# One chunk of 512 query columns instead of two of 256 at the end of a two-layer attention and mixer kernel

## The chip, the cores and the metric

The kernel runs on one core of a Trainium2 chip. The metric is the time of one execution in microseconds of device time; lower is better. The core has five engines that this text speaks of: TensorE (PE in the profile, its weight loads PEld), VectorE (DVE), ScalarE (ACT), GpSimd (POOL) and SyncE (SP), which issues most transfers.

## What is computed

Two equal layers over an input of 2048 rows by 448 columns. Each layer is a 16-head attention block (head size 28) and a mixer with an MLP, both with layer norms and residuals. Cut to what matters:

```
def _A_ref(x, wqkv, wo):
    q, k, v = heads(x @ wqkv)
    scores = jnp.einsum("bhqd,bhkd->bhqk", q, k) * (Dh ** -0.5)
    p = _softmax(scores, axis=-1)
    o = jnp.einsum("bhqk,bhkd->bhqd", p, v)
    return merged(o) @ wo
def _B_ref(x, w1, w2, w3, w4):
    h = _gelu(_layernorm(x) @ w1)
    hs = shifted_by_rows(h) @ w2      # column groups shifted by -1, +1, -2, +2 rows
    x1 = x + hs
    return x1 + _gelu(_layernorm(x1) @ w3) @ w4
for layer in range(2):
    x = x + _A_ref(_layernorm(x), A_wqkv, A_wo)
    x = x + _B_ref(_layernorm(x), B_w1, B_w2, B_w3, B_w4)
```

The weights are the same in both layers; w3 is 448 by 1792, w4 1792 by 448.

## The kernel before

**Tiles and chunks.** The 2048 rows are 16 tiles of 128. The queries of a layer are cut into chunks of tiles by `CHUNKS` (line 542): three chunks of four tiles (512 columns), then two of two tiles (256 columns): tiles 12 and 13, and 14 and 15. The 16 heads are four head groups g of four heads j. `ORDER` (line 543) lists pieces of attention work, each a chunk with a range of key tiles; a piece times a head group is a segment, and there are 68 of them (32 in layer one, 36 in layer two). A chunk whose keys are cut into several pieces spills its partial sums to DRAM (`uscr`) between them; the last chunks are done in one piece.

**Blocks.** A segment is a row of blocks. A block is one bank of PSUM, 128 keys by 512 values: one key tile by 512 queries, or two key tiles by 256 queries (line 668). A layer has 1024 blocks whatever the chunks. `t_scores` (line 1629) lets TensorE write the scores of two or three blocks at a time into banks 0 to 2 and 3 to 5, `t_exp` (line 1740) lets ScalarE take one exponential over those banks (line 1754), and `t_pv` (line 1768) multiplies by the values into bank 7, whose content VectorE copies out at the end of the segment (line 1838, or 1840 where a partial sum is read back).

**Blocks on VectorE.** Some blocks are not given to ScalarE: VectorE computes their exponential by a polynomial in eight instructions (`d_first`, line 1582, and `d_chain`, line 1595). `ahead_of` (line 1640) chooses such a block some key tiles ahead of the stream, if a quota per pair of segments allows it (`R_RATE`, line 552, `D_RATE`, line 564), if VectorE's planned load is under a threshold (`XPAR` keys 'dt'), and if a buffer is free: two of `yd`, three of `fb`, four of `PD`, and some more in unused slots of `vaug`. These extra ones in layer two are open until the segment `XSHUT` = 4 * (number of pieces) - 7 = 61 starts (line 558; `t_extra`, line 1543); after that the same space, with slots of `kT`, can hold the hidden values of an MLP group (`h2W`, line 2152).

**Behind a chunk.** `t_norm` (line 1824) divides by the softmax sums: for most chunks through DRAM (SyncE sends sums, a reciprocal by VectorE, four transfers back), for the last chunk of layer two by small matmuls (`PENORM`, line 597). `t_outproj` (line 1904) applies wo. `t_mixA` (line 1968) norms, transposes and applies w1 with a gelu. `t_mixB` (line 2124) does an MLP group of `BGROUPS` (line 545): the token mix of each tile with w2 (`t_mixB1`, which needs its two neighbours' w1 results, so that groups lag a tile behind chunks), norm, transpose, w3 with a gelu; `t_w4` (line 2224) applies w4, and `t_store` (line 2248) sends the result out. Layer two's groups are tiles 0 to 2, 3 to 6, 7 to 10, 11 and 12, and 13 to 15, one for each chunk.

**Three forms of gelu.** ScalarE's exponential and its gelu need different tables. In the middle, the first gelu is made from a tanh, which shares the table of the exponential, with steps on VectorE and GpSimd (line 2030), and the MLP's gelu is saved up: VectorE copies w3's result out of PSUM (line 2196) and one long gelu runs over the whole group between two table loads (line 2220). For the last chunk of layer two (`direct`) and for whatever comes behind the last exponential (the event "tail"), ScalarE takes the gelu straight from PSUM (lines 2000 and 2192), the transposes are done by TensorE (line 1078) instead of by DMA, and the hidden values of a direct group lie in `PT`, the tile of the exponentials.

**Order.** Nothing is ordered by hand. Every step is a generator with a priority (`RANK`, line 562, smaller goes first; segments have priority 0 and 1), and a planner in the kernel (`Sched`, line 185) simulates the engines with rough costs and writes out each engine's instruction list: the instruction that can start first, then by priority. Each engine then runs its list in that order. `XPAR` (line 575) says among others for some steps whether GpSimd (0), VectorE (1) or the earlier one (2) does them. Where TensorE would be idle for long, the planner puts in filler matmuls (line 2267) to keep its clock up.

Of the kernel before, what the change touches and what calls it, by code (L numbers as in the profile page):

```python
# [538 lines left out]
        return max(self.cur.values())  # L539


CHUNKS = {0: [(0, 4), (4, 4), (8, 4), (12, 2), (14, 2)], 1: [(0, 4), (4, 4), (8, 4), (12, 2), (14, 2)]}
ORDER = {0: [(0, 0, 4), (1, 0, 4), (0, 4, 8), (0, 8, 16), (1, 4, 16), (2, 0, 16), (3, 0, 16), (4, 0, 16)], 1: [(0, 0, 7), (1, 0, 7), (0, 7, 11), (1, 7, 11), (0, 11, 16), (1, 11, 16), (2, 0, 16), (3, 0, 16), (4, 0, 16)]}
KC = {0: [(0, 4), (4, 4), (8, 4), (12, 4)], 1: [(0, 3), (3, 4), (7, 4), (11, 2), (13, 3)]}
BGROUPS = {0: [[[0, 1, 2]], [[3, 4, 5, 6]], [[7, 8, 9, 10]], [[11, 12]], [[13, 14, 15]]], 1: [[[0, 1, 2]], [[3, 4, 5, 6]], [[7, 8, 9, 10]], [[11, 12]], [[13, 14, 15]]]}
TR_T = 2.6
TRL_T = 5.4
PVB = 2
DPRIO = 2.5
DST = [0.2, 0.2, 0.336, 0.2, 0.336, 0.336, 0.2]  # L550
# [1820 lines left out]
```

## Time and profile before

| | us |
|---|---|
| median of two runs | 1025.47 (1025.05 to 1025.9) |
| the profiled execution | 1025.66 |
| its span, first to last instruction | 1023.9 |
| ScalarE busy | 973.6 (95%) |
| of it exponentials, 791 instructions | 877.8 |
| TensorE busy, fillers included | 973.4 (95%) |
| VectorE busy | 843.5 (82%) |
| GpSimd busy | 220.1 (21%) |
| mean granted TensorE clock | 1.000 of full speed |

A row of a group shows the line, the engine, the operation, the tile written and read with their shapes, the count, and behind the bar the busy time with the mean of one in ns, then the idle time ahead of it and who ended it. Rows of a timeline start with the start and the length in us. A row of stretches shows from and to, the length, and busy time and count for PE, PEld, DVE, ACT and POOL (or for the engine of one line alone), then the granted clock, the DMA share and GB/s.

### The profile page before, as it was taken

What the parts mean: (1) busy time and instruction counts of PE and PEld (TensorE: products, weight loads), DVE (VectorE), ACT (ScalarE), POOL (GpSimd) and SP (SyncE); (2) the same over time, 40 slices, a digit from 0 to 9 for tenths busy, and PEclk for the clock granted to TensorE, in tenths of its full rate; (3) what the DMA queues carried; (4) which work ended last, traced back from release to release, by engine and by line L of the source; (5) the groups of instructions that cost most, each with busy time, mean ns of one, the idle gap of its engine ahead of it and who ended that gap; (6) DMA issues with size and microseconds to landing.
All of it is one profiled execution on the core that took longest, in us unless ns stands there. A gap on an engine that the chain in (4) does not pass through costs nothing.

```text
span 1023.9 us, 36349 instructions
## 1 busy us (share of the span) xinstructions
PE 973.4 (95%) x16102; PEld 404.7 (40%) x16102; DVE 843.5 (82%) x2134; ACT 973.6 (95%) x897; POOL 220.1 (21%) x350
## 2 busy tenths in 40 slices
PE   8999899999999999999999999999999999999998
PEld 4333344334343334344344333333333333444465
DVE  8879999988768778897788888997898888788752
ACT  6899999999999999999999999999999999999942
POOL 4003022143213013350212010112332200331220
PEclk9999999999999999999999999999999999999999
DMA  4534228121203113321133024324311110220000
GB/s 126 130 74 140 59 76 216 34 44 37 33 18 84 43 49 88 51 39 19 36 87 63 22 76 140 112 80 112 74 29 33 32 55 13 55 61 17 13 21 25
DMA packets 98829, 64.43 MB, mean 63 GB/s; under 512 B 70832, under 2 KB 87552, under 8 KB 98672
## 3 DMA queue, kind: packets, MB, share of 16 engines
q1 hardware_dynamic: 94176, 53.11, 21.1%
q0 software_dynamic: 3376, 8.09, 3.0%
q8 instruction: 126, 2.06, 0.9%
q10 hardware_dynamic: 1120, 0.92, 0.3%
q14 instruction: 31, 0.25, 0.1%
HBM read 28.16 MB, written 16.76 MB: 44 GB/s over the span
## 4 chain that ended last, share of the span: by engine, by line
ACT 62%; PE 23%; DVE 12%; DMA 1%; issue 1%; ACTq 0%; SPq 0%; DVEq 0%
ACT PT L1754 55%; PE ps L840 12%; PE ps L1487 5%; PE ps L831 4%; ACT h2T L2220 3%; PE ps L2267 1%; ACT fb L2036 1%; DVE yd L1584 1%; DMA xT<-xnd 1%; DVE fb L1619 1%; DVE fb L1615 1%; DVE PD L1624 1%; DVE ub L1840 1%; DVE vaug L1621 1%; ACT L1754 1%
## 5 line engine op out<-in xcount | busy, mean ns | idle before, releaser
L1754 ACT ACTIVATE PT<-ps 128x1024 bf16<-128x1024 f32 (+1 forms) x791 | 877.8, 1288 | 7.8 <-PE ps L1487 6.6
L1487 PE MATMUL ps<-qT,kT 32*128 32x512 bf16 (+1 forms) x2560 | 310.1, 340 | 23.5 <-ACT PT L1754 17.7
L831 PE MATMUL ps<-PT,vaug 128*32 128x512 bf16 (+1 forms) x2396 | 243.8, 341 | 0.5 <-ACT PT L1754 0.3
L1487 PEld LDWEIGHTS ps<-qT,kT 32*128 32x128 bf16 x2560 | 79.7, 91 | 292.0 <-ACT PT L1754 262.9
L840 PE MATMUL ps<-xT,w 128*32 128x512 bf16 (+3 forms) x2592 | 178.7, 343 | 1.7 <-issue 0.8
L2267 PE MATMUL ps<-ident 128*32 128x256 bf16 x2508 | 123.0, 280 | 2.2 <-POOL ident L930 1.5
L831 PEld LDWEIGHTS ps<-PT,vaug 128*32 128x32 bf16 x2396 | 71.8, 94 | 91.5 <-issue 78.2
L840 PE MATMUL ps<-w,h2T 128*32 128x448 bf16 x1288 | 89.5, 355 | 2.0 <-ACT h2T L2220 2.0
L840 PEld LDWEIGHTS ps<-xT,w 128*32 128x32 bf16 (+1 forms) x2592 | 68.9, 95 | 52.5 <-issue 25.1
L2267 PEld LDWEIGHTS ps<-ident 128*32 128x32 bf16 x2508 | 73.1, 98 | 25.3 <-issue 9.2
L1584 DVE TENSOR_SCALAR yd<-ps 128x512 int16<-128x512 f32 x94 | 64.5, 686 | 21.8 <-PE ps L1487 21.1
L1865 POOL TENSOR_TENSOR otn<-ub,fb 128x512 bf16<-128x512 f32 (+1 forms) x32 | 37.2, 1162 | 189.3 <-DMA fb<-rscr 178.7
L2196 DVE CAST h2T<-ps 128x384 bf16<-128x384 f32 (+1 forms) x84 | 52.0, 619 | 19.7 <-PE ps L840 17.9
L1615 DVE TENSOR_TENSOR fb<-fb 128x512 bf16<-128x512 int16 x112 | 49.0, 438 | 0.7
L840 PEld LDWEIGHTS ps<-w,h2T 128*32 128x32 bf16 x1288 | 34.6, 96 | 31.0 <-issue 12.0
L831 PE MATMUL ps<-PD,vaug 128*32 128x512 bf16 (+1 forms) x146 | 43.9, 342 | 1.2 <-DVE PD L1624 1.0
L840 PE MATMUL ps<-xT,wk_pad 128*32 128x512 bf16 (+1 forms) x512 | 41.2, 369 | 1.8 <-DVE kT L1226 1.2
L2267 PE MATMUL ps<-ident,xn 128*32 128x256 bf16 x896 | 40.8, 274 | 0.6 <-DVE ub L1840 0.6
L840 PE MATMUL ps<-wo_pad,otn 128*32 128x448 bf16 x512 | 36.9, 355 | 3.2 <-DVE x_res L1920 1.7
L1621 DVE TENSOR_TENSOR yd<-yd,fb 128x512 int16<-128x512 int16 x88 | 38.3, 436 | 1.2
L840 PE MATMUL ps<-wv,xT 128*32 128x448 bf16 x480 | 37.7, 356 | 0.6 <-ACT kT L1227 0.2
L840 PE MATMUL ps<-xT,wq_pad 128*32 128x512 bf16 x448 | 36.8, 382 | 1.4 <-DVE kT L1226 0.8
(238 smaller groups left out, 1318.0 us busy)
## 6 DMA issues: line engine op xcount, KB each, us to landing
uscr<-ub SPq DMA_DIRECT2D x28, 256.0 KB
ub<-uscr SPq DMA_DIRECT2D x28, 256.0 KB
fb<-rscr SPq DMA_DIRECT2D x96, 64.0 KB, 2.1
xnd<-xn SPq DMA_DIRECT2D x28, 128.0 KB, 3.1
x_res<-in_A_x_dram POOLq DMA_DIRECT2D x16, 224.0 KB, 3.3
xd<-x_res SPq DMA_DIRECT2D x16, 224.0 KB, 2.3
x_res<-xd SPq DMA_DIRECT2D x16, 224.0 KB, 4.1
out_dram<-obf SPq DMA_DIRECT2D x16, 112.0 KB, 1.8
```

Source lines behind the costliest of these rows:

```text
L831: return lambda e: e.matmul(out=out, lhsT=lhsT, rhs=rhs, start=start, stop=stop, **kw)
L840: r.append(e.matmul(out=out[c:c + w, :], lhsT=lhsT[:, c:c + w], rhs=rhs, start=start, stop=stop, tile_position=(0, c)))
L1487: yield op("pe", (0.005 + NW * 0.00042) / nc_, lambda e, i=i, kc=kc, j=j, g=g, a=a, NW=NW, bank=bank: e.matmul(out=ps[:, bank, i * NW:(i + ...
L1584: yield op("dve", c_ps(512), lambda e: e.tensor_scalar(out=y.bitcast(I16)[:, 0:512], in0=ps[:, bi(bank), :], scalar1=SCALE * L2E * FS, sca ...
L1615: yield op("dve", D_[2], lambda e: e.tensor_tensor(out=z, in0=qa, in1=qa, op=ALU.mult), reads=fk, writes=fk, urge=urge, two=True)
L1619: yield op("dve", D_[4], lambda e: e.tensor_tensor(out=z, in0=z, in1=w, op=ALU.mult), reads=yk + fk, writes=fk, urge=urge, two=True)
L1621: yield op("dve", D_[5], lambda e: e.tensor_tensor(out=ya, in0=ya, in1=z, op=ALU.add), reads=yk + fk, writes=yk, urge=urge, two=True)
L1754: yield op("act", 0.0635 + n * w * 0.000833, lambda e, bk=bk, s0=s0, n=n, w=w: e.activation(out=PT[:, s0:s0 + n, 0:w], in_=ps[:, bk[0]:bk[ ...
L1865: yield both(("eo", L, ch), 0.2 + NW * 0.0021, 0.07 + NW * 0.00104, lambda e: e.tensor_tensor(out=otn[:, g, 0:NW], in0=u, in1=rb[:, 0:NW], ...
L2196: ev = op("dve", c_ps(m * NW), lambda e, hr=hr, pv=pv: e.tensor_copy(out=hr, in_=pv), reads=[("ps", bi(b))], writes=hk, touch=[b])
L2220: yield op("act", c_act(len(fr_) * NW), lambda e, v=v: e.activation(out=v, in_=v, func=ACT.Gelu_apprx_tanh), reads=allk, writes=allk, tab= ...
L2267: return [e.matmul(out=ps[32 * c:32 * c + 32, bi(b), 0:256].rearrange("p (a n) -> p a n", n=128), lhsT=xn[:, 0, D:D + 32] if live else ide ...
```

## The change

Layer two's last two chunks become one of four tiles, and its last two MLP groups both hang on it. `PENORM` and `direct` follow the last chunk, so they now hold for tiles 12 to 15 and for both groups. `ORDER` loses a piece, so there are 64 segments, and `XSHUT` becomes 57. The core of the diff:

```
-CHUNKS = {0: [(0, 4), (4, 4), (8, 4), (12, 2), (14, 2)], 1: [(0, 4), (4, 4), (8, 4), (12, 2), (14, 2)]}
-ORDER = {0: [(0, 0, 4), (1, 0, 4), (0, 4, 8), (0, 8, 16), (1, 4, 16), (2, 0, 16), (3, 0, 16), (4, 0, 16)], 1: [(0, 0, 7), (1, 0, 7), (0, 7, 11), (1, 7, 11), (0, 11, 16), (1, 11, 16), (2, 0, 16), (3, 0, 16), (4, 0, 16)]}
+CHUNKS = {0: [(0, 4), (4, 4), (8, 4), (12, 2), (14, 2)], 1: [(0, 4), (4, 4), (8, 4), (12, 4)]}
+ORDER = {0: [(0, 0, 4), (1, 0, 4), (0, 4, 8), (0, 8, 16), (1, 4, 16), (2, 0, 16), (3, 0, 16), (4, 0, 16)], 1: [(0, 0, 7), (1, 0, 7), (0, 7, 11), (1, 7, 11), (0, 11, 16), (1, 11, 16), (2, 0, 16), (3, 0, 16)]}
-BGROUPS = {0: [[[0, 1, 2]], [[3, 4, 5, 6]], [[7, 8, 9, 10]], [[11, 12]], [[13, 14, 15]]], 1: [[[0, 1, 2]], [[3, 4, 5, 6]], [[7, 8, 9, 10]], [[11, 12]], [[13, 14, 15]]]}
+BGROUPS = {0: [[[0, 1, 2]], [[3, 4, 5, 6]], [[7, 8, 9, 10]], [[11, 12]], [[13, 14, 15]]], 1: [[[0, 1, 2]], [[3, 4, 5, 6]], [[7, 8, 9, 10]], [[11, 12], [13, 14, 15]]]}
-R_RATE = {(0,): 0, (1,): 0.006, (2,): 0.016, (3,): 0.04, (4,): 0.006, (5,): 0.051, (6,): 0.059, (7,): 0, (8,): 0.06, (9,): 0.048, (10,): 0.024, (11,): 0.15, (12,): 0.066, (13,): 0.022, (14,): 0.022, (15,): 0.192, (16,): 0.233, (17,): 0.075, (18,): 0.115, (19,): 0.273, (20,): 0.093, (21,): 0.233, (22,): 0.355, (23,): 0.29, (24,): 0, (25,): 0.268, (26,): 0.146, (27,): 0.207, (28,): 0.183, (29,): 0.243, (30,): 0.071, (31,): 0.163, (32,): 0.241, (33,): 0.078}
+R_RATE = {(0,): 0, (1,): 0.16, (2,): 0.016, (3,): 0.04, (4,): 0.09, (5,): 0.051, (6,): 0.102, (7,): 0.137, (8,): 0.062, (9,): 0.048, (10,): 0.024, (11,): 0.133, (12,): 0.096, (13,): 0.07, (14,): 0.022, (15,): 0.192, (16,): 0.282, (17,): 0.075, (18,): 0.115, (19,): 0.273, (20,): 0.09, (21,): 0.233, (22,): 0.066, (23,): 0, (24,): 0, (25,): 0.33, (26,): 0.146, (27,): 0, (28,): 0.183, (29,): 0.243, (30,): 0.071, (31,): 0.043, (32,): 0.241, (33,): 0.078}
-D_RATE = {(0,): 0, (1,): 0.177, (2,): 0, (3,): 0.517, (4,): 0.133, (5,): 0.289, (6,): 0.447, (7,): 0.362, (8,): 0.067, (9,): 0.088, (10,): 0.129, (11,): 0.262, (12,): 0, (13,): 0.687, (14,): 0.003, (15,): 0.526, (16,): 0, (17,): 0.061, (18,): 0.049, (19,): 0.1, (20,): 0.403, (21,): 0.327, (22,): 0.258, (23,): 0, (24,): 0.164, (25,): 0.165, (26,): 0.245, (27,): 0, (28,): 0.523, (29,): 0.61, (30,): 0.121, (31,): 0.077, (32,): 0.657, (33,): 0.301}
+D_RATE = {(0,): 0, (1,): 0.36, (2,): 0, (3,): 0.517, (4,): 0.133, (5,): 0.289, (6,): 0.111, (7,): 0.588, (8,): 0.1, (9,): 0.088, (10,): 0.129, (11,): 0.262, (12,): 0.106, (13,): 0.687, (14,): 0.081, (15,): 0.526, (16,): 0.109, (17,): 0.061, (18,): 0.049, (19,): 0.1, (20,): 0.403, (21,): 0.156, (22,): 0.143, (23,): 0.214, (24,): 0.32, (25,): 0.276, (26,): 0, (27,): 0.048, (28,): 0.523, (29,): 0.61, (30,): 0.121, (31,): 0.077, (32,): 0.657, (33,): 0.301}
```

A quota of r for a pair of segments allows r * 4 blocks for each key step of a segment, so that the sums over segments follow from these lines. "Order sought anew" is the rest: 24 of the ranks (among them the MLP group of chunk 2 from 2.447 to 2.958, its token mix from 1.159 to 2.518, the MLP of chunk 3 from 2.996 to 1.112, its mixer from 2.129 to 1.466), two of the lead times `Q_LEAD`, and entries of `XPAR`: 'l2' from 16 to 14 (w3 and w4 are loaded earlier), the engine of 31 small steps, and thresholds of VectorE's and TensorE's planned load. Of those, 'dt' rises for ten of the groups of four segments (0.628 to 0.873 in the second) and falls for four (2, 9, 11 and 12), and 'wt', the planned idle share of TensorE from which ScalarE's two-bank calls become three-bank calls, rises in most.

More of the change, by code (lines that the diff above doesn't have):

```diff
@@ L563 @@
-Q_LEAD = {(0, 1): 7, (0, 2): 102, (0, 3): 50, (1, 0): 86, (1, 1): 54, (1, 2): 9, (1, 3): 71}
-D_RATE = {(0,): 0, (1,): 0.177, (2,): 0, (3,): 0.517, (4,): 0.133, (5,): 0.289, (6,): 0.447, (7,): 0.362, (8,): 0.067, (9,): 0.088, (10,): 0.129, (11,): 0.262, (12,): 0, (13,): 0.687, (14,): 0.003, (15,): 0.526, (16,): 0, (17,): 0.061, (18,): 0.049, (19,): 0.1, (20,): 0.403, (21,): 0.327, (22,): 0.258, (23,): 0, (24,): 0.164, (25,): 0.165, (26,): 0.245, (27,): 0, (28,): 0.523, (29,): 0.61, (30,): 0.121, (31,): 0.077, (32,): 0.657, (33,): 0.301}
+RANK = {('q', 0, 1): 2.187, ('q', 0, 2): 1.163, ('q', 0, 3): 2.532, ('q', 1, 0): 1.046, ('q', 1, 1): 2.224, ('q', 1, 2): 2.603, ('q', 1, 3): 1.838, ('b', 0, 0): 2.786, ('b', 0, 1): 2.168, ('b', 0, 2): 1.786, ('b', 0, 3): 2.946, ('b', 0, 4): 2.347, ('b', 1, 0): 2.813, ('b', 1, 1): 2.272, ('b', 1, 2): 2.958, ('b', 1, 3): 1.112, ('b', 1, 4): 1.2, ('a', 0, 0): 1.465, ('a', 0, 1): 1.069, ('a', 0, 2): 2.66, ('a', 0, 3): 1.27, ('a', 0, 4): 2.52, ('a', 1, 0): 2.44, ('a', 1, 1): 2.086, ('a', 1, 2): 1.987, ('a', 1, 3): 1.466, ('a', 1, 4): 2.296, ('k', 0, 1): 2.195, ('k', 0, 2): 2.331, ('k', 0, 3): 1.257, ('k', 1, 0): 2.95, ('k', 1, 1): 2.469, ('k', 1, 2): 2.057, ('k', 1, 3): 1.894, ('k', 1, 4): 1.325, ('c', 0, 0): 2.53, ('c', 0, 1): 1.436, ('c', 0, 2): 2.421, ('c', 0, 3): 2.418, ('c', 0, 4): 2.923, ('c', 1, 0): 1.772, ('c', 1, 1): 1.73, ('c', 1, 2): 2.518, ('c', 1, 3): 1.26, ('c', 1, 4): 2.718, ('w', 0, 0): 3, ('w', 0, 1): 2.526, ('w', 0, 2): 2.67, ('w', 0, 3): 2.228, ('w', 0, 4): 2.959, ('w', 1, 0): 1.616, ('w', 1, 1): 2.347, ('w', 1, 2): 2.397, ('w', 1, 3): 1.705, ('w', 1, 4): 1.73, ('o', 0, 0): 2.913, ('o', 0, 1): 2.031, ('o', 0, 2): 2.592, ('o', 0, 3): 1.459, ('o', 0, 4): 2.576, ('o', 1, 0): 1.548, ('o', 1, 1): 1.29, ('o', 1, 2): 2.296, ('o', 1, 3): 1, ('o', 1, 4): 2.51, ('v', 0, 1): 1, ('v', 0, 2): 2.093, ('v', 0, 3): 2.749, ('v', 1, 0): 2.464, ('v', 1, 1): 2.494, ('v', 1, 2): 1.411, ('v', 1, 3): 1, ('v', 1, 4): 2.679, ('l', 1, 0): 2.0, ('l', 1, 1): 1.613, ('l', 1, 2): 2.72, ('l', 1, 3): 2.152, ('l', 1, 4): 1.196}
@@ new lines @@
+Q_LEAD = {(0, 1): 7, (0, 2): 96, (0, 3): 50, (1, 0): 85, (1, 1): 54, (1, 2): 9, (1, 3): 71}
+D_RATE = {(0,): 0, (1,): 0.36, (2,): 0, (3,): 0.517, (4,): 0.133, (5,): 0.289, (6,): 0.111, (7,): 0.588, (8,): 0.1, (9,): 0.088, (10,): 0.129, (11,): 0.262, (12,): 0.106, (13,): 0.687, (14,): 0.081, (15,): 0.526, (16,): 0.109, (17,): 0.061, (18,): 0.049, (19,): 0.1, (20,): 0.403, (21,): 0.156, (22,): 0.143, (23,): 0.214, (24,): 0.32, (25,): 0.276, (26,): 0, (27,): 0.048, (28,): 0.523, (29,): 0.61, (30,): 0.121, (31,): 0.077, (32,): 0.657, (33,): 0.301}
```

3 lines of the change are left out of this document (1 added, 2 removed).

## Prediction

> **What bounds the kernel now.** I read the page's busy times first, then ScalarE's groups and its idle time, then the busy times by stretch, then the ends of the last segments on VectorE, and last the timeline behind the last exponential.
>
> ```profile
> PE 973.4 (95%) x16102; PEld 404.7 (40%) x16102; DVE 843.5 (82%) x2134; ACT 973.6 (95%) x897; POOL 220.1 (21%) x350
> ACT  6899999999999999999999999999999999999942
> ACT 62%; PE 23%; DVE 12%; DMA 1%; issue 1%; ACTq 0%; SPq 0%; DVEq 0%
> L1754 ACT ACTIVATE PT<-ps 128x1024 bf16<-128x1024 f32 (+1 forms) x791 | 877.8, 1288 | 7.8 <-PE ps L1487 6.6
> 851.20:916.60 65.40, 62.22 (x1185) 27.95 (x1177) 52.20 (x122) 65.34 (x59) 19.80 (x31) 1.00 0.19 44
> 916.60:971.00 54.40, 51.94 (x939) 24.29 (x938) 44.74 (x119) 54.38 (x54) 9.50 (x18) 1.00 0.09 19
> 971.00:1024.00 53.00, 49.19 (x1161) 31.48 (x1154) 19.67 (x41) 19.55 (x29) 6.35 (x15) 1.00 0.08 25
> ```
>
> Two regimes follow each other. Up to 970.5 us ScalarE is full (54.38 of 54.40 us in the last stretch; the columns are PE, PEld, DVE, ACT, POOL), and its 791 exponentials waited only 7.8 us in all. There only work taken from ScalarE shortens the run. Behind 971 ScalarE works 19.55 us of 53, and TensorE 49.19: that tail is a matter of TensorE's work and of the chain of small steps that feeds it.
>
> The ends of the segments show the pace. Each row is the copy that ends one head group: 64 blocks in the 512 form, 32 in the 256 form.
>
> ```profile
> 761.53 0.69 DVE L1838 COPY ub<-ps 128x512 f32<-128x512 f32 x1 [0.17 <-PE ps L831]
> 851.24 0.69 DVE L1838 COPY ub<-ps 128x512 f32<-128x512 f32 x1
> 916.61 0.41 DVE L1838 COPY ub<-ps 128x256 f32<-128x256 f32 x1
> 970.95 0.42 DVE L1838 COPY ub<-ps 128x256 f32<-128x256 f32 x1 [0.47 <-PE ps L831]
> ```
>
> ```profile
> 864.25 1.28 ACT L2220 ACT_TABLE_LOAD   x1
> 865.54 6.18 ACT L2220 ACTIVATE h2T<-h2T 128x7168 bf16<-128x7168 bf16 x1
> 871.74 1.28 ACT L1754 ACT_TABLE_LOAD   x1
> 945.98 0.54 ACT L2036 ACTIVATE fb<-fb 112x256 f32<-112x256 f32 x1
> 946.29 7.90 ACT L1754 ACTIVATE PT<-ps 128x1024 bf16<-128x1024 f32 x7
> 970.47 1.28 ACT L2192 ACT_TABLE_LOAD   x1
> 971.77 0.60 ACT L2192 ACTIVATE kT<-ps 128x512 bf16<-128x512 f32 x1
> ```
>
> **The change part by part.** The sum starts from the profiled execution, 1025.66 us with a span of 1023.9; that is 0.19 above the median of 1025.47.
>
> *Half as many, wider matmuls: 0.* The two chunks had 2 x 128 blocks of exponentials, the one has 256. The 256 form takes 916.61 to 970.95, 54.3 us for 128 blocks; the 512 form takes 761.53 to 851.24 for three segments (192 blocks, with one session of gelus in it). ScalarE is the bound in both and its banks stay 512 wide, so the TensorE time saved lies beside it. That is 54.3 / 128 = 0.42 us a block, and (89.7 - 9) / 192 = 0.42 with an estimated 9 us for the session (the one at 864.25 takes 8.8). The next digit bounds it: about 1 us either way. The Trainium skill ("TensorE: Matmul & The Clock Gate", Back-to-back issue gap) puts a fixed 2.5 ns on each matmul; the change saves 256 for scores and 256 for values, by the page an estimated 1.3 us of TensorE, and the sum would be 1.3 lower if that engine set the pace. The rows above say that it doesn't.
>
> *Tanh that leaves the exponential stretch: -1.3 us.* Tiles 12 and 13 had their first gelu as four tanh calls (L2036) among the exponentials; now all four tiles take the direct form behind them. One starts at 945.98 and the next exponential at 946.29: 0.31 net, four are 1.25. Bounds -2.2 (four times the whole 0.54) and -1.2.
>
> *The tail: +6.8 us.* Behind the last exponential now lie output projection, mixer and norms of tiles 12 to 15, not only of 14 and 15, and the token mix of 11 and 12.
>
> ```profile
> 971.43 0.61 PE L831 MATMUL ps<-e,ub 128*128 128x4 f32 x4 [0.31 <-DVE ub L1838]
> 973.74 1.71 PE L840 MATMUL ps<-wo_pad,otn 128*32 128x448 bf16 x32
> 974.81 1.38 DVE L1920 TENSOR_TENSOR x_res<-x_res,ps 128x448 f32<-128x448 f32 x2 [0.55 <-PE ps L840]
> 976.11 1.15 DVE L1050 BATCH_NORM_STATS2 st<-x_res 128x6 f32<-128x448 f32 x2
> 978.55 0.51 DVE L1065 TENSOR_SCALAR xn<-x_res,mv,mst 128x448 bf16<-128x448 f32 x1 [1.08 <-POOL mst L1945]
> 980.72 0.62 PE L1089 MATMUL ps<-ident,xn 128*128 128x128 bf16 x8
> 982.23 1.92 PE L840 MATMUL ps<-xT,w 128*32 128x256 bf16 x64
> 989.84 2.45 PE L840 MATMUL ps<-w,hT 112*32 112x448 bf16 x48
> 991.96 1.27 DVE L2105 SCALAR_TENSOR_TENSOR x1b<-x_res,mst,ps 128x448 f32<-128x448 f32 x2 [1.14 <-PE ps L840]
> 992.11 5.42 PE L840 MATMUL ps<-xT,w 128*32 128x256 bf16 x192
> 1000.36 9.28 PE L840 MATMUL ps<-xT,w 128*32 128x384 bf16 x224
> 1012.88 8.12 PE L840 MATMUL ps<-w,PT 128*32 128x448 bf16 x168
> 1021.12 0.68 DVE L2251 SCALAR_TENSOR_TENSOR obf<-x_res,shf,ps 128x448 bf16<-128x448 f32 x1 [1.97 <-PE ps L840]
> ```
>
> TensorE gains: projection of two more tiles 1.71 (32 matmuls at 973.74); w1 at 512 instead of 256 columns 1.92 (982.23); token mix of two tiles 1.63 (two thirds of 2.45); transposes for two tiles in the mixer and two in the MLP, which the direct form does on TensorE, 2 x 0.62; the normalising by matmul of twice as many columns about 1.2 (twice the 0.61 and what follows it up to 973.74, some of it latency). That is 7.7. The tail's TensorE is idle 53 - 49.19 = 3.8 us, of which 2.9 lie behind the last matmul (1021.0 to 1023.9); 0.9 can be filled: 6.8. Lower bound: the 1.2 of the normalising hides too: 5.6. Upper bound: nothing covers VectorE's longer chain. Two more tiles add 1.38 + 1.15 + 2 x 0.51 there, and about 5 us in the second norm (1.27 for two at 991.96, the rest alike): 8.6, with the 7.7 some 16. I take the low side, because there is cover: the last MLP layer of tiles 7 to 10, four tiles at 1.97 + 0.68 = 2.65 us each (the spacing in the row of 1021.12), 10.6 us of TensorE work without a predecessor in the chunk. What is lost as cover is the MLP of 11 and 12: its 5.42 us at 992.11 ran while 13 to 15 were normed; now it needs the new chunk's mixer itself. The two MLP groups share the tile PT, so 13 to 15 cannot write it until 11 and 12 are read; TensorE has them in that order anyway: 0.
>
> *VectorE freed: -2.3 us.* VectorE takes some blocks from ScalarE. In the stretch 851 to 971 it loses the work of tiles 12 and 13: projection, statistics and norm (1.38 + 1.15 + 1.02 by the rows above), the same again for the second norm of 11 and 12, the mixer's evacuations and tanh steps (1.7 + 1.6 and as much again as the latter), and the steps of the normalising (four reciprocals and copies, an estimated 2 us): 14 us. One block costs it 0.69 + 0.44 + 0.44 (rows below), a fourth pass like the last two and four short ones of 0.29: an estimated 3.2 us. That is between four and five blocks; I take five, since its idle time there (22.9 us, below) adds room. ScalarE pays 877.8 / (2048 - 134) = 0.46 us for a block. Bounds: 0 if the planner takes none, -2.3 if five.
>
> ```profile
> L1584 DVE TENSOR_SCALAR yd<-ps x94: 674/685/693, 60.5 to 954.7; 128x512 int16<-128x512 f32 x94
> L1584 DVE TENSOR_SCALAR vaug<-ps x40: 656/686/693, 40.4 to 861.2; 128x512 int16<-128x512 f32 x40
> L1584 DVE TENSOR_SCALAR vaug<-ps 128x512 int16<-128x512 f32 x10 | 6.8, 684 | 1.2 <-PE ps L1487 1.0
> L1615 DVE TENSOR_TENSOR fb<-fb 128x512 bf16<-128x512 int16 x112 | 49.0, 438 | 0.7
> L1621 DVE TENSOR_TENSOR yd<-yd,fb 128x512 int16<-128x512 int16 x88 | 38.3, 436 | 1.2
> L1611 DVE TENSOR_SCALAR fb<-yd x88: 222/286/757, 61.4 to 958.7; 128x512 uint16<-128x512 uint16 x88
> L2005 DVE TENSOR_SCALAR hT<-ps 112x256 bf16<-112x256 f32 x4 | 1.7, 423 | 0.8 <-PE ps L840 0.8
> L2035 DVE SCALAR_TENSOR_TENSOR fb<-fb,hT 112x256 f32<-112x256 f32 x4 | 1.6, 406 | 0.0
> 0.00:485.00 485.00, 45.22 (x66) 1.00 0.30 72
> ```
>
> *Scratch that closes sooner: +2.3 us.* 94 + 40 = 134 blocks go to VectorE. The 40 used extra scratch in the tile vaug, the last at 861.2, which is where segment 61 (`XSHUT`) starts. With 64 segments instead of 68 the same formula gives 57, the second segment of chunk 2, about 761. Between, ten blocks went through it (third row, 750 to 859). I take half of them as lost: 5 x 0.46. Bounds 0 (the two fixed buffers suffice) and 4.6.
>
> *Order sought anew: -2.8 us.* Ranks and engine choices move work that ScalarE hides; what counts is the number of VectorE's blocks. Summed over the segments of the diff, layer one's quotas grow from 290 to 326 (12%), the four segments (1, 1, 7..11) and the four (1, 1, 11..16) shrink from 53 to 21. 66 of the 134 blocks lie in layer one (last row, up to 485 us): 12% more are 8; I take off 2 for those eight segments: net 6 x 0.46. No row shows what a quota yields, so the bounds are wide: -8 (17 blocks, 54 us of VectorE's 1023.9 - 843.5 = 180 idle) and +4.
>
> *Queues.* SyncE loses chunk 3's normalisation through DRAM (six transfers for each head group) and four DMA transposes; what it still queues at the end are the stores, from two buffers as before. GpSimd gains the power steps of two more tiles in the tail, inside the chain already priced: 0.
>
> Sum: 1025.66 - 1.3 + 6.8 - 2.3 + 2.3 - 2.8 = 1028.4, given as 1028.
>
> **The rivals.** *The gelu of 7 to 10 falls among the exponentials (slower).* Its fourteenth evacuation landed at 971.77, 1.3 us behind the last exponential, so its gelu ran for nothing in the tail. With VectorE freed it can be ready sooner; then ScalarE pays a session as at 864.25 to 873.02, 8.8 us, and the tail loses its cover. Result 1028.4 + 8.8 - 1.2 = 1036 while the chain holds (the tail at its lower bound), up to 1028.4 + 8.8 + 9.2 = 1046 when nothing covers it. It decides as soon as that evacuation comes before the last exponential. For it: the 14 us freed. Against: its evacuations run from the middle of the stretch to the very end even with gaps on VectorE. The Trainium skill ("ScalarE: Activation LUTs", What ACT_TABLE_LOAD costs) counts a drain of 1380 ns with each load of 1283; the trace agrees on 1.28, but the gelu starts 1.29 us after its load, with no drain between; by the page the session would be 2.7 us dearer.
>
> *VectorE takes much more (faster).* 22.9 us of 119.8 are idle in the two stretches (119.8 - 52.20 - 44.74); with 14 freed that is 12 blocks instead of five, and 17 in the rest by the bound: 1028.4 - 3.2 - 5.2 = 1020. For over 2% it would need some 45 blocks beside those five and six, 144 us of the 180 idle: hardly.
>
> *VectorE takes many fewer.* If the new plan gives up forty of the 134 blocks, 18 us: 1047 and above. For it: less scratch and lower quotas in layer two. Against: VectorE is idle for 180 us in all, and the change crowds it nowhere.
>
> *TensorE's clock.* The columns behind show 1.00 granted in every stretch. If the longer chain leaves TensorE without work for some microseconds and the clock halves for one such spell, about 3 us are lost: 1031. The Trainium skill ("TensorE: Matmul & The Clock Gate", Part 1) states a half-rate clock after an idle window of 3.4 us; no run here shows one.
>
> **How the numbers follow.** The forecast has 0.57. All its low ends together give 1019, all high ends 1049; the high ones have separate causes, so its own range is 1019 to 1039, half of the way up. The gelu among the exponentials 0.22 (1036 to 1047, a third of it over 2%), VectorE more 0.13 (0.05 over 2%), fewer 0.06, the clock 0.02. Two per cent is 20.5 us, about what a measurement of this kernel can tell from no change. Slower 0.14, faster 0.05, within 0.81. The range 1015 to 1044 leaves out the ends of the rivals.
>
> **What would show it.** Right: the last exponential ends at 966 to 970, the tail behind it is 58 to 61 us long (53.4 now), TensorE is over 90% busy there; about 135 to 142 blocks on VectorE; no vaug row of L1584 behind 765; the 512 form's four segments end 26 to 27 us apart. Wrong: a gelu session in the last 110 us before the last exponential, a tail of 65 us or one of under 54, or fewer than 120 blocks.

## The result and the profile after

| | before | after |
|---|---|---|
| median, us | 1025.47 (two runs) | 1036.76 (two runs: 1034.19 and 1039.33) |
| ratio, 95% interval | | 1.0107 [1.0082, 1.0132] |
| profiled execution; its span, us | 1025.66; 1023.9 | 1039.33; 1037.6 |
| start of the last chunk (end of the segment before it), us | 851.24 | 851.02 |
| last exponential ends, us | 970.45 | 974.42 |
| tail behind it, us | 53.45 | 63.18 |
| mean granted clock of the profiled execution | 1.000 | 0.992 |

The change costs 11.3 us, 1.1%. The profiled execution lies 2.6 above the median of its two runs; the sums below are made against it, 13.7 us of span. Up to the last chunk 0.2 us are gained, 4.2 are lost among the last chunk's exponentials, and 9.7 in the tail. The other run of the result had a mean clock of 0.998 and took 5.1 us less; no profile of it is kept.

The ends of the segments after (VectorE's timeline; start and length):

```profile
851.02 0.69 DVE L1838 COPY ub<-ps 128x512 f32<-128x512 f32 x1
...
887.01 0.68 DVE L1838 COPY ub<-ps 128x512 f32<-128x512 f32 x1
...
921.41 0.69 DVE L1838 COPY ub<-ps 128x512 f32<-128x512 f32 x1 [0.80 <-PE ps L831]
...
948.94 0.69 DVE L1838 COPY ub<-ps 128x512 f32<-128x512 f32 x1 [0.41 <-PE ps L831]
```

The first of the four segments holds the gelu session of tiles 3 to 6 (8.8 us), as the stretch before had it, so 36.0 is 27.2 without it. The second is 34.4 us long, the third 27.5 and the fourth 26.0. The second holds the four tanh calls of tiles 7 to 10 (0.52 each), which explains 2.1 us of the difference and no more. The profile's row of the granted clock, one digit for each fortieth of the span, shows one low place, and stretches around that place and around 140 us say more:

```profile
PEclk9999999999999999999999999999999999799999
```

```profile
136.50:140.00 3.50, 1.81 (x31) 0.64 (x23) 3.40 (x7) 3.50 (x4) 1.26 (x1) 1.00 0.15 53
140.00:143.50 3.50, 3.13 (x29) 0.81 (x29) 2.68 (x7) 1.23 (x2) 0.00 (x0) 0.51 0.16 16
886.00:891.00 5.00, 4.92 (x62) 2.39 (x63) 4.56 (x14) 5.00 (x5) 0.00 (x0) 1.00 0.39 98
891.00:904.70 13.70, 13.70 (x102) 4.25 (x94) 7.32 (x17) 10.52 (x10) 1.04 (x1) 0.50 0.09 26
904.70:910.00 5.30, 5.30 (x74) 1.89 (x71) 2.34 (x7) 4.72 (x5) 1.22 (x1) 1.00 0.01 2
```

TensorE runs at half rate for 3.4 us from 140.1 and for 13.7 us from 891.0. The profile before has no such spell (other runs of that kernel were granted 0.997 to 1.000). In the second spell ScalarE is busy 10.52 of 13.70 us. Its timeline shows what it waits for:

```profile
898.45 1.02 ACT L1754 ACTIVATE PT<-ps 128x1024 bf16<-128x1024 f32 x1 [0.43 <-PE ps L1487]
899.96 1.02 ACT L1754 ACTIVATE PT<-ps 128x1024 bf16<-128x1024 f32 x1 [0.49 <-PE ps L1487]
901.48 1.45 ACT L1754 ACTIVATE PT<-ps 128x1536 bf16<-128x1536 f32 x1 [0.50 <-PE ps L1487]
...
918.97 55.45 ACT L1754 ACTIVATE PT<-ps 128x1536 bf16<-128x1536 f32 x50
```

The scores (L1487) come too late. The bracket understates the loss: two calls in flow overlap, so a two-bank call takes 0.90 from start to start (before: 954.20 to 955.10), here 1.51 (898.45 to 899.96). Worked out over the nine calls of the last chunk that a wait follows, start to start against 0.90 for two banks and 1.33 for three, the waits cost 5.4 us; the idle time alone is 4.0. Seven of the nine lie in the spell and cost 4.7. The other two, at 912 and 969 us, cost 0.7; the run with more filler (below) has the one at 969 too, without that spell.

The tail, as one stretch of each kernel (before, then after):

```profile
970.45:1023.90 53.45, 49.68 (x1169) 31.81 (x1169) 19.75 (x42) 20.08 (x30) 6.79 (x15) 1.00 0.09 25
```

```profile
974.42:1037.60 63.18, 59.41 (x1300) 36.32 (x1294) 27.75 (x61) 21.27 (x31) 12.52 (x25) 1.00 0.06 19
```

TensorE's idle time is the same, 3.77 us in both; its busy time grows by 9.73. Its groups by shape in these stretches, before:

```profile
L840 PE MATMUL ps<-xT,w 128*32 128x256 bf16 x272 | 8.4, 273 | 0.0
...
L840 PE MATMUL ps<-w,hT 112*32 112x448 bf16 x48 | 2.4, 352 | 0.0
...
L840 PE MATMUL ps<-wo_pad,otn 128*32 128x448 bf16 x32 | 1.7, 355 | 0.0
L2267 PE MATMUL ps<-ident 128*32 128x256 bf16 x36 | 1.7, 274 | 0.0
L1089 PE MATMUL ps<-ident,xn 128*128 128x128 bf16 x20 | 1.6, 221 | 0.0
```

and after:

```profile
L840 PE MATMUL ps<-xT,w 128*32 128x512 bf16 x72 | 5.3, 380 | 0.0
...
L840 PE MATMUL ps<-w,hT 112*32 112x448 bf16 x80 | 4.3, 353 | 0.0
...
L840 PE MATMUL ps<-wo_pad,otn 128*32 128x448 bf16 x64 | 3.4, 354 | 0.0
L1089 PE MATMUL ps<-ident,xn 128*128 128x128 bf16 x36 | 3.1, 221 | 0.8 <-DVE xn L1070 0.8
L2267 PE MATMUL ps<-ident 128*32 128x256 bf16 x52 | 2.6, 275 | 0.0
L831 PE MATMUL ps<-rT,selq 8*128 8x128 f32 x8 | 1.4, 296 | 0.0
L831 PE MATMUL ps<-e,ub 128*128 128x4 f32 x8 | 1.1, 255 | 0.0
L1881 PE MATMUL ps<-identf,rs 128*8 128x128 f32 x4 | 0.8, 274 | 0.0
```

Projection, token mix and transposes grew by 1.7, 1.9 and 1.5, the normalising (last three rows, 3.3) by 1.6 over its 1.7 before, w1 by 1.7 (one run of 64 matmuls in the timeline, 1.92 before, 3.63 after). New are 24 matmuls of w3 of tiles 7 to 10, about 1.4 us (72 of the 512-wide kind, of which w1 has 48), and 16 fillers more, 0.9. w4 has 504 matmuls in both. The groups overlap at their edges, so their 10.7 stand for the 9.73.

The order put w3 of 13 to 15 ahead of most of w4 of 11 and 12 (TensorE's timeline after):

```profile
1011.67 0.75 PE L840 MATMUL ps<-w,PT 128*32 128x448 bf16 x12
...
1013.27 9.29 PE L840 MATMUL ps<-xT,w 128*32 128x384 bf16 x224
1022.38 12.28 PE L840 MATMUL ps<-w,PT 128*32 128x448 bf16 x256
```

Both groups share `PT`, and no step of the kernel makes the second group wait until the first is read. Only 24 matmuls of w4, six hidden chunks of tile 11, ran ahead of w3 of 13 to 15. So in the changed kernel w4 multiplies tile 12 in all of its 14 hidden chunks, and tile 11 in 8 of them, with hidden values of 13 to 15: these two tiles of the output are not what the reference computes. The instructions are the same in number and size, and a run below (an own tile) shows that the times don't hang on it.

### The profile page after: what moved, and what is told of

Read it like the earlier page. It is cut to its first block, busy times and chain, and to the rows that moved or that the text cites. A ratio compares the mean times of both kernels' runs of the same rounds, so it can differ in the third digit from the quotient of the medians.

```text
span 1037.6 us, 35673 instructions
## 1 busy us (share of the span) xinstructions
PE 991.7 (96%) x15803; PEld 405.5 (39%) x15806; DVE 848.6 (82%) x2143; ACT 973.8 (94%) x897; POOL 187.1 (18%) x315
## 4 chain that ended last, share of the span: by engine, by line
ACT 66%; PE 28%; DVE 5%; DMA 0%; issue 0%; ACTq 0%; DVEq 0%
ACT PT L1754 60%; PE ps L840 15%; PE ps L1487 7%; PE ps L831 5%; ACT h2T L2220 3%; PE ps L2267 2%; ACT L1754 1%; ACT fb L2036 1%; ACT L2220 0%; DMA PT<-in_A_wqkv_dram 0%; ACT hT L2018 0%; DVE fb L1617 0%; DVE fb L1615 0%; DVE fb L2035 0%; DVE qT L1288 0%
## 5 line engine op out<-in xcount | busy, mean ns | idle before, releaser
L1487 PE MATMUL ps<-qT,kT 32*128 32x512 bf16 (+1 forms) x2304 | 314.5, 362 | 20.9 <-ACT PT L1754 14.8
L1487 PEld LDWEIGHTS ps<-qT,kT 32*128 32x128 bf16 x2304 | 78.6, 91 | 294.4 <-ACT PT L1754 262.3
L831 PEld LDWEIGHTS ps<-PT,vaug 128*32 128x32 bf16 x2155 | 66.9, 95 | 89.0 <-issue 75.9
L1584 DVE TENSOR_SCALAR yd<-ps 128x512 int16<-128x512 f32 x104 | 71.3, 687 | 21.8 <-PE ps L1487 20.6
L840 PEld LDWEIGHTS ps<-xT,w 128*32 128x32 bf16 x2528 | 66.1, 95 | 54.5 <-issue 25.3
L840 PE MATMUL ps<-w,h2T 128*32 128x448 bf16 x1008 | 71.2, 360 | 2.4 <-ACT h2T L2220 2.4
L1865 POOL TENSOR_TENSOR otn<-ub,fb 128x512 bf16<-128x512 f32 (+1 forms) x24 | 30.4, 1265 | 195.4 <-DMA fb<-rscr 185.6
L2196 DVE CAST h2T<-ps 128x512 bf16<-128x512 f32 (+1 forms) x70 | 44.3, 633 | 18.4 <-PE ps L840 17.4
L840 PE MATMUL ps<-xT,wq_pad 128*32 128x512 bf16 x512 | 43.0, 389 | 3.0 <-DVE yd L1584 2.0
L840 PE MATMUL ps<-xT,wk_pad 128*32 128x512 bf16 (+2 forms) x512 | 39.3, 362 | 2.8 <-DVE kT L1226 1.9
L1619 DVE TENSOR_TENSOR fb<-fb,yd 128x512 bf16<-128x512 bf16 x94 | 39.6, 425 | 0.8
L1056 POOL TENSOR_SCALAR rstd<-mv 128x1 f32<-128x1 f32 (+2 forms) x21 | 5.6, 266 | 187.1 <-DVE mv L1051 187.1
```

Of the source, the lines that this page charges most:

```text
L831: return lambda e: e.matmul(out=out, lhsT=lhsT, rhs=rhs, start=start, stop=stop, **kw)
L840: r.append(e.matmul(out=out[c:c + w, :], lhsT=lhsT[:, c:c + w], rhs=rhs, start=start, stop=stop, tile_position=(0, c)))
L1487: yield op("pe", (0.005 + NW * 0.00042) / nc_, lambda e, i=i, kc=kc, j=j, g=g, a=a, NW=NW, bank=bank: e.matmul(out=ps[:, bank, i * NW:(i + ...
L1584: yield op("dve", c_ps(512), lambda e: e.tensor_scalar(out=y.bitcast(I16)[:, 0:512], in0=ps[:, bi(bank), :], scalar1=SCALE * L2E * FS, sca ...
L1619: yield op("dve", D_[4], lambda e: e.tensor_tensor(out=z, in0=z, in1=w, op=ALU.mult), reads=yk + fk, writes=fk, urge=urge, two=True)
L1865: yield both(("eo", L, ch), 0.2 + NW * 0.0021, 0.07 + NW * 0.00104, lambda e: e.tensor_tensor(out=otn[:, g, 0:NW], in0=u, in1=rb[:, 0:NW], ...
```

## The experiments

Each time is a median beside runs of the kernel before on the same chip. The first four shared one chip (before 1025.66, nine runs), the next four a second (1026.61, eleven), the last had a third (1025.58, nine).

**The changed kernel again** (no edit).

> The changed kernel, nothing edited, to see what the granted clock does from run to run. In it tile 12 in all 14 hidden chunks and tile 11 in 8 of 14 are multiplied with the hidden values of tiles 13 to 15, which have overwritten theirs in PT. Theory A (the tail): 1034 in runs whose mean clock is 0.998 or more, about 1039 in runs with a spell of half rate in the last chunk, and never below 1032, since the tail alone costs 9.8 us. Rival C (the clock makes the loss): runs without any spell are within 3 us of the kernel before.

Measured 1037.82 (five runs, 1036.74 to 1042.50), ratio 1.0129 [1.0108, 1.0150]. The profiled run has the same two spells, the last exponential at 974.6 and a tail of 63.2. Its five runs order by their clock: 0.997, 0.995 and 0.995 at 1036.7 to 1037.8, 0.992 at 1039.5, 0.989 at 1042.5. That fits theory A, but none of the five was without a spell, so rival C was not tried here; the run at full clock further below (five blocks more, 1036.65) speaks against it.

**The chunk alone**: the kernel before with the new `CHUNKS`, `ORDER` and `BGROUPS`, and so with before's ranks, quotas and thresholds.

> The four-tile chunk with all ranks, quotas, thresholds and engine choices of the kernel before. Theory A (the loss is moved work and an uncovered chain in the tail): slower than before by at least the 9.8 us of the tail, 1036 to 1044, because the order was only sought to repair the structure; last exponential within 2 us of 970.4, tail 63 us or longer. Rival B (the order sought anew is at fault): at or below 1033, faster than the changed kernel.

Measured 1043.73, ratio 1.0180 [1.0163, 1.0197], worse than with the new order. Clock 0.998, last exponential at 970.5, but a tail of 71.4, with 136 fillers in it (the tail as a stretch, then the group of the fillers):

```profile
970.50:1042.00 71.50, 64.38 (x1428) 39.61 (x1418) 28.66 (x62) 21.93 (x33) 11.60 (x24) 1.00 0.05 17
```

```profile
L2267 PE MATMUL ps<-ident 128*32 128x256 bf16 x136 | 4.4, 273 | 0.0
```

So the loss is there without the new order, and it is in the tail. How much of it is the structure and how much the numbers, which were sought for two chunks, this run does not tell. The new order takes 8 us of the tail back, there and not, as I had it, among the exponentials.

**The order alone**: after's numbers with the two chunks of 256.

> Two chunks of 256 as before, with all ranks, quotas, thresholds and engine choices of the changed kernel. Theory A: the last exponential within 2 us of 970.4, since the changed kernel shows the same 851 us up to the last chunk as the kernel before; the tail has numbers sought for another structure and may be 4 to 15 us longer than 53.4, so 1028 to 1042. Rival B (the order is at fault): the last exponential is 4 us or more late, and the loss of 11 us stands in front of it.

Measured 1038.94, ratio 1.0130 [1.0113, 1.0148]; clock 0.997, last exponential at 972.1, tail 66.3, all within theory A's ranges. There all of w3 of 7 to 10 lies behind the last exponential (224 matmuls of 512 columns, 13.2 us). The numbers fit only the structure that they were sought for, so this run says little of "the order" as a cause of its own.

**Less late work**: w3, gelu and w4 of tiles 11 and 12 in layer two use 2 of their 14 hidden chunks (about 9.6 us of TensorE work left out).

```
+nf_ = 2 if (L == 1 and tiles[0] == 11) else 14
-for fch in range(14):
+for fch in range(nf_):
```

> The changed kernel with only 2 of the 14 hidden chunks computed for tiles 11 and 12 in the last MLP (48 column-matmul groups of w3 and 24 of w4 are left out, 5.1 and 4.5 us of TensorE by the spacing of 0.107 and 0.19 us a group; that part of the output is left out). Everything up to the last exponential is the same. Theory A: the second half of the tail is bound by TensorE's work, so 8.5 to 9.6 us shorter, 1025 to 1028. Rival D (the second half is bound by the chain of tiles 13 to 15): under 4 us shorter, 1031 or more.

Measured 1030.17, ratio 1.0048 [1.0029, 1.0067]; tail 57.3, 5.9 less, between what the two theories said. 128 fillers (5.1 us) stand in the tail, where the changed kernel has 52 (2.6). w3 of 13 to 15 starts 37.2 us behind the last exponential instead of 38.9: to there the chain normalise, project, mix and norm, of four tiles, is nearly as long as the work; only the w4 of 11 and 12 that had stood behind it came off in full. The four runs also give the clock's price in one kernel: 1028.44 and 1029.10 at 1.000, 1031.24 at 0.995, 1032.66 at 0.993.

**Less cover**: w4 of tiles 7 to 10 uses 2 of 14 hidden chunks (about 9.1 us left out), the work that I had named as cover.

> The changed kernel with only 2 of the 14 hidden chunks taken in the last matmul of tiles 7 to 10 (48 column-matmul groups, 9.0 us of TensorE at 0.1875 us a group, are left out, and that part of the output). The groups run in the first half of the tail. Theory A2 (what sets the tail up to the MLP of 13 to 15 is the chain of four tiles: normalising, projection, norm, transposes, w1, token mix, second norm): the tail stays within 2.5 us of 63.2. Theory A (the tail is TensorE's work throughout): 9 us shorter, about 54.

Measured 1038.16 (two runs), ratio 1.0111 [1.0081, 1.0142]; tail 61.3, only 1.9 less. In its place stand 232 fillers, and TensorE waits for the norms (its groups by shape in the tail):

```profile
L2268 PE MATMUL ps<-ident 128*32 128x256 bf16 x232 | 8.4, 274 | 0.0
...
L1089 PE MATMUL ps<-ident,xn 128*128 128x128 bf16 x36 | 3.4, 221 | 2.4 <-DVE xn L1065 1.2 <-DVE xn L1070 0.9
```

The cover did its work: without it the chain is there with nearly its full length (theory A2). Up to w3 of 13 to 15 chain and work of the new tail are within 2 us of each other, so taking away work there gives little.

**Some filler behind the normalising**: four matmuls of 128x256 behind each of the four small normalising matmuls of a head group in the last chunk.

```
+[e.matmul(out=ps[...], lhsT=ident[:, 32 * c:32 * c + 32], rhs=ident..., ...) for c in range(4 if L == 1 and n == 4 else 0)]
```

> The changed kernel with the same planned order; behind each of the four small matmuls that turn the softmax sums (four for each head group of the last chunk) four filler matmuls of 256 columns are issued into unused columns of the same bank. It tests whether the half-rate spell at 891 us comes from a stretch in which TensorE is issued only tiny matmuls. If so: no spell in the last chunk, mean clock 0.997 or 0.998 (the short spell near 140 us stays), 1033 to 1035. Rival (the spell comes from elsewhere, or by chance): spells as before, clock 0.989 to 0.997, 1036 to 1039.

Measured 1040.41, ratio 1.0138 [1.0112, 1.0163], clock 0.989 in the profiled run. Both theories named lower times. The spell at 891 is gone, and one of the same length stands behind the next segment's end (919.61), as two stretches show; a third, of 3.4 us, follows at 957.5, and the one near 140 lasts 6.8 us here:

```profile
919.00:923.40 4.40, 4.35 (x57) 2.17 (x58) 3.15 (x7) 4.23 (x5) 0.69 (x3) 1.00 0.23 68
923.40:937.10 13.70, 13.56 (x97) 4.90 (x89) 6.29 (x17) 9.66 (x9) 3.01 (x4) 0.50 0.10 20
```

**An own tile**: the same, and the hidden values of 11 and 12 in `h2T` instead of `PT`, so that each group has its own.

```
+elif direct and tiles[0] == 11:
+    hname = yield ("acq", ["h2T"])
+    hb, hkey = h2T, [[("h2T", f), ("xst",)] for f in range(14)]
```

> As the run before, and the hidden values of tiles 11 and 12 get a tile of their own (h2T, free by then) instead of sharing PT with those of 13 to 15, so that the planner may place the two groups without regard to each other and nothing is overwritten. Theory A2: the chain to 13 to 15 is the same, so the tail is 61 to 63 us against 63.2. Rival E (the shared tile cost the tail its length): under 58 us.

Measured 1044.58, ratio 1.0194 [1.0155, 1.0233], at clocks of 0.979 to 0.992. The tail is 64.3, and 64.3 with the shared tile and the same filler: sharing costs the tail nothing. The clock fell in six spells of the profiled run, which took 1054.38; that the total is higher than in the run before is put down to them.

**Five blocks more**: the edit with some filler, and the thresholds of the last group of segments opened ('dt' 15 to 1.0, 'ft' 15 to 0): 139 blocks on VectorE instead of 134.

> As e6, with the two thresholds that let VectorE take a block in the last chunk opened ('dt' 15 from 0.577 to 1.0, 'ft' 15 from 0.146 to 0), which makes 139 blocks out of 134; the rest of the last chunk is planned anew by that. By the price in the prediction the last exponential is 5 x 0.46 = 2.3 us earlier than in e6 and the tail is as long, so 2 us faster. Rival (VectorE has no room left there, its steps are late for others): the last exponential is less than 1 us earlier, or the tail longer by as much.

Measured 1038.28 (1036.21 to 1044.71), ratio 1.0132 [1.0096, 1.0167]. The profiled run, 1036.65, had no spell at all: span 1034.7, clock 1.000, last exponential at 969.45, tail 65.2. The median is the forecast 2 us below that of some filler, but the two ranges of runs overlap, so the five blocks are priced from the traces, further below.

**More filler**: twelve such matmuls instead of four, and twelve times as many in one filler slot at 137 us.

> The changed kernel with more filler matmuls at the two places where its clock fell: twelve (128x256) behind each of the four small normalising matmuls per head group in the last chunk, and twelve times as many in one filler slot at about 137 us, just ahead of the wait for VectorE. The planned order stays. Theory C (the half-rate spells cost the exponential stretch 4 us, and the rest of the loss is the tail): the clock is 0.998 or more, the last exponential ends at 969 to 971.5 us, the tail stays at 62.5 to 64.5, the time is 1033 to 1036, ratio 1.007 to 1.010. Rival B (the stretch is late by the new order itself, and the spells lie beside a wait that is there anyway): the clock is 0.998 or more, but the last exponential still ends at 973.5 to 975.5, the time is 1037 to 1039. Rival F (a filler of any size does not help, the clock falls with the total load or by chance): the clock stays at 0.989 to 0.996 with spells behind the segment ends, the time is 1037 to 1042.

Measured 1042.17, ratio 1.0162 [1.0148, 1.0176]; in the profiled run a clock of 0.998 and both spells gone (the other four had 0.993 to 0.998). None of the three theories had it right: the last exponential still ends at 974.21, which speaks for B, but ScalarE now waits at the fillers themselves (its timeline), and the tail is 65.2 with them in it:

```profile
890.64 12.81 ACT L1754 ACTIVATE PT<-ps 128x1536 bf16<-128x1536 f32 x12 [1.38 <-PE ps L1487]
...
921.29 1.02 ACT L1754 ACTIVATE PT<-ps 128x1024 bf16<-128x1024 f32 x1 [0.83 <-PE ps L1487]
922.92 8.50 ACT L1754 ACTIVATE PT<-ps 128x1536 bf16<-128x1536 f32 x8 [0.61 <-PE ps L1487]
...
952.05 22.15 ACT L1754 ACTIVATE PT<-ps 128x1536 bf16<-128x1536 f32 x20 [1.10 <-PE ps L1487]
```

Counted start to start as above, its waits in the last chunk (a fifth, of 0.92 us, belongs to a spell of 3.4 us at 928) cost 6.1 us; taken off, the last exponential would end at 968.1. The same account for the changed kernel gives 974.42 - 5.4 - 1.1 = 967.9; the 1.1 is the spell at 140, for here the segment before the last chunk ends at 849.96 instead of 851.02. The run with five blocks more, which has no spell there either, is ahead by about as much, 1.2 us, up to 728 us (728.29 against 729.47); it loses it again at 746 to 750 us, where ScalarE waits for scores. That the two sums agree supports theory C; it is worked out, for no run has the changed order at full clock without added fillers. The cure costs more than the spells: by medians it is 4.4 us slower than the changed kernel in its five further runs.

## Why the prediction was right and wrong

The time fell into the range of 1015 to 1044 and within 2%, 9 us above the 1028: a loss of 11 us where 3 were forecast. That it lies in the range is owed to the range's width, not to the sum. Of the signs named, TensorE's share in the tail (94%) and the last `vaug` row (748.8 us) came; the last exponential at 974, the tail of 63 and the 134 blocks all lie outside what I had called right. The sign of a gelu session in the last 110 us was badly set, since the session at 864 in the kernel before has it too. Against the profiled execution before, by the prediction's steps:

| step | predicted | measured |
|---|---|---|
| tanh leaves the exponentials | -1.3 | -1.2 (four steps of 0.31; the calls are gone) |
| VectorE freed, scratch, order sought anew | -2.8 | about -1.3 (849.96 against 851.24, see below) |
| tail | +6.8 | +9.7 |
| TensorE's clock, with two waits behind the spell | 0 | +6.5 (4.7, 0.7 and 1.1), worked out |
| sum | +2.7 | +13.7 |

*Wider matmuls: right.* The four segments were not all 26 to 27 us long as forecast; the fourth was, with 26.0. But without the gelu session (8.8), the tanh calls (3.3 before, 2.1 after) and the waits (5.4 after), the last 256 blocks, 13 and 14 of them on VectorE, took 107.1 us before (851.24 to 970.45) and 107.2 after (851.02 to 974.42).

*VectorE and the order: the sum was 1.5 us off, its terms were wrong.* I priced all three in blocks: five more, five lost, six more, and that the sum came near is luck. The net was none, 134 before and 134 after: 66 became 69 in layer one (up to 485 us), 55 became 51 from there to 851 us, 13 became 14 behind. By tile they were 94 + 40 and are now (VectorE's groups after)

```profile
L1584 DVE TENSOR_SCALAR yd<-ps 128x512 int16<-128x512 f32 x104 | 71.3, 687 | 21.8 <-PE ps L1487 20.6
L1584 DVE TENSOR_SCALAR vaug<-ps 128x512 int16<-128x512 f32 x30 | 20.3, 686 | 4.7 <-PE ps L1487 4.5
```

The scratch closed as forecast, and its blocks went through `yd`. VectorE's freed time bought one block, since the planner's threshold, not its time, was the limit. With the threshold opened five came, and the price held: without its waits (2.3 us) the stretch from 851.26 to 969.45 takes 115.9, with 134 blocks (849.96 to 974.21, less 6.1) 118.1, so 2.2 us for five; but the tail grew by 0.9 over the kernel with the same filler, as w3 of 7 to 10 came later. What the order did gain, 1.3 us, lies ahead of the last chunk (849.96 against 851.24 at full clock) and came without more blocks there (121 before, 120 after); which of its numbers brought it was not tried.

*The tail: the step that failed in size.* Its list of moved work was right: projection 1.7 (1.71 forecast), token mix 1.9 (1.63), w1 1.7 (1.92), transposes 1.5 (1.24), normalising 1.6 (1.2). Three things are missing. The 0.9 of idle time was not filled: it is 3.77 in both, with 0.8 of it now in waits for the second norm (the L1089 row after). 0.9 of fillers came on top, which I had counted as work neither before nor after. And 1.4 us of w3 of tiles 7 to 10 slid behind the last exponential, which I had thought done. The cover that I named covers (less cover: 9.1 us of it are worth 1.9), and the claim that 13 to 15 cannot write `PT` until 11 and 12 are read, in an order that TensorE has "anyway", was wrong in fact, though it cost no time (own tile).

*The clock: the rival with 0.02.* Half-rate spells came, at two places that I had not looked at, among the exponentials and not in the tail, and at some 6 us instead of 3. Whole times give a slightly lower price: in less late work 13.7 us at half rate, in three spells, cost about 3.9 us (1032.66 against 1028.44 and 1029.10), which scales to 4.9 for the 17.1 us here. So the clock is 5 to 6.5 of the 13.7 us; if it is 5, 1.5 us stay unexplained. I looked for it where a longer chain might leave TensorE dry, and the profile's 95% said that it nowhere was. *The gelu of 7 to 10 among the exponentials* did not come: the session at 871.9 is that of 3 to 6, and VectorE's part of either sign came to nothing.

## What to carry to other kernels

A last chunk of twice the width moves work behind the end of the bounding engine's stretch: count all of it, with the fillers and with whatever work of earlier groups slides over that edge, and take off idle time only where something is ready to fill it. Freed time on a helper engine is worth nothing until the rule that hands it work lets more through, so read that rule's limit before the idle time. Where one engine feeds the bounding one, read its granted clock by stretch and not only its busy share: here it fell behind rows of tiny matmuls and around one wait, and the feed with it.

## What the hardware showed that I had not expected

TensorE's clock halved in stretches where the profile has it busy. In the 5.0 us ahead of 891.0 it is busy 4.92, but with operations such as these (TensorE's timeline of the changed kernel):

```profile
888.55 0.83 PE L831 MATMUL ps<-e,ub 128*128 128x4 f32 x6
889.47 0.39 PE L1487 MATMUL ps<-qT,kT 32*128 32x512 bf16 x3
...
890.70 0.28 PE L1881 MATMUL ps<-identf,rs 128*8 128x128 f32 x1
```

four columns wide, or 32 or 8 rows or columns of the array. That such operations count for little in what sets the clock is a reading; no run here isolates it. At 140.1 it was really idle: a wait for VectorE, 1.97 us from 138.4 on, is twice as long as any gap between matmuls in the kernel before (0.96). The spells last 3.4, 6.8 or 13.7 us, that is one, two or four times 3.4. The Trainium skill ("TensorE: Matmul & The Clock Gate", Part 1) lets the clock fall after a window of about 3.4 us without work and rise after a busy one; the length of the spells agrees with that window, the condition doesn't: no trace here shows 3.4 us without matmuls ahead of a fall, and the longest gap there is 2.05 us (less late work). In the profiled executions twelve fillers behind each small matmul kept the clock up at the segments' ends; four did so everywhere in one (five blocks more) and not in two others (some filler, an own tile), so one trace is no proof of a cure. Whether a given execution falls into a spell varies: the kernel with less late work had two runs at 1.000, one at 0.995 and one at 0.993, and five blocks more had the same wait at 138.3 (1.98 us) and no spell.
